# Listed orders for TensorE, ScalarE and VectorE in an attention and channel-mix kernel

## The chip, the core and the metric

The kernel runs on one core of one Trainium2 chip. The metric is the device time of one execution in microseconds (us). The time before is 232.12 us, the median of three runs (231.74 to 232.44). One further execution was recorded by the hardware profiler; it took 232.05 us, of which 230.3 us lie between its first and its last instruction (the span), and the durations in this document come from it.

A core has five engines that each take their instructions in a fixed order: TensorE (PE: matrix products, and PEld, the loads of its weights), VectorE (DVE), ScalarE (ACT), GpSimd (POOL) and SyncE (SP). In this kernel POOL does almost nothing but issue the loads, and SP issues the stores and the transposes by DMA.

## The reference

Two layers follow each other, on 8 sequences of 576 rows. The first is sliding-window attention with 8 heads of 64; the second is a channel mix that shifts each sequence by one row, with two weight matrices for a squared ReLU (512 to 1024 and back to 512) and one for a gate. All of it is computed, in float32 at the borders and bfloat16 inside.

```python
mask = (rel >= 0) & (rel < window)                       # window = 128
scores = where(mask, scale * q @ k.T + bias, -1e9)       # bias = -slope[h] * |rel|
x = softmax(scores) @ v                                  # B=8, H=8, S=576, D=64 -> (8, 576, 512)
x_prev = x shifted by one row, zeros first
xk = mu_k * x + (1 - mu_k) * x_prev
xr = mu_r * x + (1 - mu_r) * x_prev
out = sigmoid(xr @ w_r) * (relu(xk @ w_k)**2 @ w_v)
```

## The kernel before, in words

**Work.** Each batch b has four groups g of two heads. For a group TensorE makes transposes of q and k (qk_quad for batches 1 and 2, qk_some for 3 to 5; batches 6 and 7 are transposed by DMA), then scores (L729), which ScalarE turns into exponentials (L743) and VectorE multiplies with a mask (L756); then attend (L785), the product with v, which VectorE normalises (L791, L796); then a transpose back (out_t for batch 0, out_some for batches 1 to 5 at L840, DMA for 6 and 7). From the result VectorE makes xk and xr (L883, L890). The last 64 rows of each batch, its tails, are transposed apart: for batches 1 to 3 by four TensorE instructions (L915).

**The channel mix** is called 13 times, mix 0 to mix 12, each for a block of 256 to 512 rows. A mix has eight K operations (L994, four matmuls each, with ReLU on ScalarE at L1001 and the square at L967 on VectorE or L965 on ScalarE), and for every 128 rows one R operation (L1012, four matmuls, with tanh at L1019) and two V halves a and b (L1028, four matmuls each; VectorE makes the output ot from them at L1033, and SP stores it). "V mix0.0a" is the first half of the first 128 rows of mix 0. It needs the first half of w_v in wv_sb, and its half b needs the second.

**Loads.** POOL issues 113 loads in one fixed order. Counted from 0 they are: v of batch 0, w_k and parts of q and k (0 to 8), the rest of v and w_k (9 to 12), q and k of batch 1 (13 to 16) and its tails (17, 18), w_r (19), v of batch 1 (20 to 24), the halves of w_v (25, 26), q and k of batch 2 (27 to 30), its tails (31, 32) and v (33 to 37), then for every later batch q and k (38 to 45 for batch 3), tails (46, 47 for batch 3) and v.

**What sets the order.** No instruction is ordered at run time. The builder makes a list of operations with `plan.add`, each with the engines it may run on, a planned duration and latency, and the operations that it depends on. `Plan.run` plays the list through as events and emits every operation in the order of its planned start, so each engine's order, the buffer that each operation gets (`take`) and, for those that may run on ScalarE or VectorE, the engine, are settled before the kernel starts. Waits between engines are put in afterwards from the data. In `run`, a free engine takes from its ready operations the one with the smallest key. That key begins with a number of `PLACES`, one for each operation of TensorE, ScalarE and VectorE (L104 to L123). For TensorE `pe_key` changes it: while the array is split in two halves of 64 rows, operations of 64 rows go first. `paced` holds the transposes and scores of late batches until enough of the mixes has been planned. `dma` and `fab` plan the loads; `lat` is the planned latency of a transfer.

TensorE also runs 90 filler matmuls (L690) that write a scratch tile. Their key puts them behind everything else, so the plan takes them only where TensorE has nothing ready.

Of the kernel before, what the change touches and what calls it, by code (L numbers as in the profile page):

```python
# [21 lines left out]
PLACES = [int(x) for x in '''  # L22
# [54 lines left out]
'''.split()]  # L77


# [14 lines left out]
class Plan:  # L94
# [71 lines left out]
    def pe_key(self, n, rows):  # L166
        key = (n.place,) + tuple(n.prio)
# [1169 lines left out]
```

## Time and profile before

| | |
|---|---|
| median of three runs | 232.12 us |
| the profiled execution | 232.05 us, span 230.3 us |
| TensorE busy | 223.5 us (97% of the span) |
| VectorE busy | 187.7 us (82%) |
| ScalarE busy | 163.1 us (71%) |
| POOL busy | 93.9 us (41%) |
| granted TensorE clock | 1.000 |

Busy is the time in which at least one instruction of the engine is under way. A matmul's own duration is longer than the time until the next may start: a matmul of 512 columns lasts 379 ns, and the next starts 216 ns after it. So the time that an operation takes from TensorE is read from start to start, and is called its slot here. The word stall is used for slot time beyond what the same operation takes elsewhere. "Landing" is when the last part of a load has arrived.

### The profile page before, as it was taken

The page shows a single profiled execution, that of the slowest core. Times are in us where ns is not written, and L with a number is a line of the kernel's source. Part 1 is how long each engine was busy: PE and PEld are TensorE (multiplying, and loading weights), DVE is VectorE, ACT ScalarE, POOL GpSimd, SP SyncE. Part 2 cuts the span into 40 slices and gives each one's busy share as a digit, 9 for nine tenths or more (in the row PEclk, how much of TensorE's full clock was granted, in tenths as well). Part 3 has the DMA queues.
Part 4 walks back from the last instruction along what each step waited for, and adds up shares of the span by engine and source line. Part 5 has one row for each costly group of instructions (what it writes and reads, how often), then busy time and mean ns, then how long its engine had stood idle before and what let it go on. Part 6 is the DMA issues. An engine that isn't in the chain of part 4 may idle for free.

```text
span 230.3 us, 6675 instructions
## 1 busy us (share of the span) xinstructions
PE 223.5 (97%) x2715; PEld 135.2 (59%) x2715; DVE 187.7 (82%) x423; ACT 163.1 (71%) x295; POOL 93.9 (41%) x120
## 2 busy tenths in 40 slices
PE   8999998999999999999999999999999999999994
PEld 8675764765656656455655745545765544545552
DVE  8496998799949998997678997999999979563252
ACT  3769999599989969999797747959476455117421
POOL 8787654579976960991004961700000000000000
PEclk9999999999999999999999999999999999999999
DMA  6999999999999999999643999995230330231032
GB/s 169 183 168 197 189 161 198 193 176 156 189 141 170 160 145 184 96 144 185 141 117 38 173 180 156 131 136 182 78 86 3 137 103 37 89 129 52 3 137 91
DMA packets 121566, 31.11 MB, mean 135 GB/s; under 512 B 108216, under 2 KB 117696, under 8 KB 121536
## 3 DMA queue, kind: packets, MB, share of 16 engines
q0 software_dynamic: 96016, 16.26, 99.3%
q1 hardware_dynamic: 23776, 13.84, 24.0%
q10 hardware_dynamic: 1744, 0.59, 1.0%
q8 instruction: 21, 0.34, 0.6%
q14 instruction: 9, 0.07, 0.1%
HBM read 33.56 MB, written 9.44 MB: 187 GB/s over the span
## 4 chain that ended last, share of the span: by engine, by line
PE 79%; DMA 12%; POOL 4%; issue 2%; DVE 1%; ACT 0%; DVEq 0%; POOLq 0%
PE uno L994 25%; PE uno L1028 25%; PE uno L1012 13%; PE duo L785 7%; PE duo L729 6%; DMA wv_sb<-in_moe_w_v_dram 5%; DMA cb<-in_k_dram 4%; DMA wk_sb<-in_moe_w_k_dram 3%; PE uno L840 3%; POOL vs L503 1%; POOL cb L499 1%; POOL tv L508 1%; DVE ot L1033 1%; PE uno L1089 1%; DVE xr L890 0%
## 5 line engine op out<-in xcount | busy, mean ns | idle before, releaser
L994 PE MATMUL uno<-xk,wk_sb 128*128 128x256 bf16 (+2 forms) x416 | 72.4, 314 | 0.7 <-ACT qk L699 0.4
L1028 PE MATMUL uno<-wv_sb,kk 128*128 128x512 bf16 (+2 forms) x296 | 69.3, 374 | 1.1 <-DMA wv_sb<-in_moe_w_v_dram 1.0
L743 ACT ACTIVATE at<-duo 128x1024 bf16<-128x1024 f32 (+2 forms) x68 | 65.0, 1002 | 5.9 <-PE duo L729 5.5
L1001 ACT ACTIVATE rl<-uno 128x256 bf16<-128x256 f32 (+2 forms) x104 | 48.3, 496 | 25.7 <-PE uno L994 25.1
L994 PEld LDWEIGHTS <-wk_sb 128*128 128x128 bf16 x416 | 38.6, 98 | 23.4 <-issue 0.8
L503 POOL DMA_DIRECT2D vs<-in_v_dram x32 | 28.5, 906 | 40.5 <-PE duo L785 33.7
L1028 PEld LDWEIGHTS <-kk 128*128 128x128 bf16 x296 | 27.2, 98 | 29.7 <-issue 1.5
L756 DVE TENSOR_TENSOR at<-at,mask 128x1024 bf16<-128x1024 bf16 x56 | 37.2, 681 | 7.2 <-ACT at L743 7.2
L967 DVE TENSOR_TENSOR kk<-rl 128x256 bf16<-128x256 bf16 (+2 forms) x96 | 31.3, 337 | 12.5 <-ACT rl L1001 12.0
L1019 ACT ACTIVATE rs<-uno 128x512 bf16<-128x512 f32 x36 | 22.1, 617 | 21.5 <-PE uno L1012 13.2
L1012 PE MATMUL uno<-wr_sb,xr 128*128 128x512 bf16 x144 | 36.9, 380 | 0.0
L1033 DVE SCALAR_TENSOR_TENSOR ot<-rs,uno 128x512 f32<-128x512 bf16 (+2 forms) x37 | 24.2, 662 | 10.7 <-PE uno L1028 8.6
L699 ACT COPY qk<-uno 128x512 bf16<-128x512 bf16 (+1 forms) x41 | 21.8, 600 | 4.7 <-PE uno L1089 3.2
L890 DVE SCALAR_TENSOR_TENSOR xr<-dl,mu_sb,xt 128x576 bf16<-128x576 bf16 (+1 forms) x32 | 24.5, 774 | 0.0
L890 DVE SCALAR_TENSOR_TENSOR xk<-dl,mu_sb,xt 128x576 bf16<-128x576 bf16 (+1 forms) x32 | 24.4, 772 | 0.0
L785 PEld LDWEIGHTS <-at 128*128 128x128 bf16 x576 | 21.2, 98 | 5.0 <-issue 0.4
L796 DVE TENSOR_TENSOR xu<-duo,rc 128x640 bf16<-128x640 f32 x28 | 22.8, 817 | 0.9 <-DMA xt<-xu 0.5
L1012 PEld LDWEIGHTS <-xr 128*128 128x128 bf16 x144 | 13.3, 98 | 13.0
L534 POOL DMA_DIRECT2D cb<-in_k_dram x20 | 17.9, 919 | 4.9 <-DMA vs<-in_v_dram 2.9
L785 PE MATMUL duo<-vs,at 128*128 128x65 bf16 x448 | 19.0, 194 | 0.0
L534 POOL DMA_DIRECT2D cb<-in_q_dram x20 | 17.7, 938 | 0.8 <-PE uno L840 0.7
L699 ACT COPY xt<-uno 128x512 bf16<-128x512 bf16 (+3 forms) x28 | 15.2, 580 | 2.5 <-PE uno L823 1.5
(83 smaller groups left out, 202.8 us busy)
## 6 DMA issues: line engine op xcount, KB each, us to landing
out_dram<-ot SPq DMA_DIRECT2D x30, 256.0 KB, 3.3
vs<-in_v_dram POOLq DMA_DIRECT2D x32, 128.0 KB, 6.6
cb<-in_q_dram POOLq DMA_DIRECT2D x20, 128.0 KB, 6.6
cb<-in_k_dram POOLq DMA_DIRECT2D x20, 128.0 KB, 5.9
out_dram<-ot SPq DMA_DIRECT2D x10, 128.0 KB, 1.8
wk_sb<-in_moe_w_k_dram POOLq DMA_DIRECT2D x2, 512.0 KB, 7.2
cb<-in_q_dram POOLq DMA_DIRECT2D x4, 256.0 KB, 10.2
cb<-in_k_dram POOLq DMA_DIRECT2D x4, 256.0 KB, 10.5
```

Source lines behind the costliest of these rows:

```text
L503: return dma(POOL, 256, issue_t(1024), lambda e: nc.gpsimd.dma_start(out=vs_buf[h.idx][:, j, :, 0:D], in_=v[b, :, 128 * j:128 * j + 128].r ...
L534: return [dma(POOL, 256, issue_t(1024), lambda e, r=r: nc.gpsimd.dma_start(out=cb_buf[h.idx][:, i, r], in_=src[:, :, r]), [g], kind="q") f ...
L699: (nc.scalar.copy if e == ACT else nc.vector.tensor_copy)(out=out, in_=in_)
L743: lambda e, ah=ah, w=w, hp=hp: nc.scalar.activation(out=ah(), in_=two(hp)[:, :, 0:w], func=AF.Exp, scale=float(scale)), (), [hp])
L756: nc.vector.tensor_tensor(out=a, in0=a, in1=m, op=ALU.mult)
L785: nc.tensor.matmul(a[:, hl, t - t0], lhsT=at[:, lo:lo + 128], rhs=vs[:, u, 2 * g + hl, :] if u < NF else tvb[:, 2 * g + hl], start=(u == u ...
L890: lambda e: nc.vector.scalar_tensor_tensor(out=buf[hk.idx][:, g, e0 + c0:e0 + c1], in0=dls(), scalar=mu[:, g:g + 1], in1=xc(1), op0=ALU.mu ...
L967: nc.vector.tensor_tensor(out=out, in0=in_, in1=in_, op=ALU.mult)
L994: nc.tensor.matmul(one(hp)[:, 0:n], lhsT=wk_sb[:, po, 128 * fo:128 * fo + 128], rhs=xk_buf[hx.idx][:, po, c0:c1], start=(po == 0), stop=(p ...
L1001: a = op(ACT, act_t(n), [s], pr, lambda e, hp=hp, hr=hr: nc.scalar.activation(out=rl_buf[hr.idx][:, 0:n], in_=one(hp)[:, 0:n], func=AF.Rel ...
L1012: nc.tensor.matmul(one(hp), lhsT=xr_buf[hx.idx][:, po, 128 * c:128 * c + 128], rhs=wr_sb[:, po], start=(po == 0), stop=(po == NPO - 1))
L1028: nc.tensor.matmul(one(hv)[:, a:b], lhsT=kk_buf[hk.idx][:, fo, o:o + 128], rhs=wv_sb[:, fo, a:b], start=(fo == 0), stop=(fo == NFO - 1))
```

## The change

`PLACES` is replaced by `ORDER`, three lists of operation numbers: 425 for TensorE, 303 for ScalarE, 420 for VectorE, together 1148, numbered in the order of the calls of `plan.add` for these engines. `add` looks up the engine and the position of each operation, so that the engine of an operation that may run on two is given as well. In `run`, a free engine of these three may take only the operation whose position is its next turn; when that one isn't ready, the engine stays idle in the plan. `pe_key` and `paced` go. The fillers are in the list like any other operation.

In the plan, the landing of a POOL load is moved by a constant that depends on its number: -0.6 us for the first seven, +0.5 to +1.6 us for the next 35, +0.5 us for all later ones. POOL's and SP's order is still by `prio`, and the list of operations, their instructions and their data are the same. All of this is settled while the kernel is built.

```diff
+ORDER = {
+    "PE": [int(x) for x in """
+48 128 57 58 68 53 50 69 45 64 46 39 43 72 61 76 75 60 67 55 56 41 70 59 54 65 131 52 62 47 44 77 144 133 146 66
...
     def add(self, engs, dur, lat, deps, prio, emit=None, need=(), free=()):
         engs = (engs,) if isinstance(engs, str) else engs
+        place = None
+        if engs[0] in ORDER:
+            e, place = self.places[self.placed]
+            assert e in engs
+            engs = (e,)
+            self.placed += 1
...
-        n.place = 0
-        if emit is not None and engs[0] in ("PE", "ACT", "DVE"):
-            if prio[0] < 1e11:
-                n.place = PLACES[self.placed]
-                self.placed += 1
-            else:
-                n.place = 1 << 40
+        n.place = place
...
-    def pe_key(self, n, rows):
-        key = (n.place,) + tuple(n.prio)
-        if rows == 64 and n.rows[0] == 64:
-            return (-1e8,) + tuple(key)
...
-                    if e == "PE":
-                        cand.sort(key=lambda n: self.pe_key(n, rows))
+                    if e in turn:
+                        cand = [n for n in cand if n.place == turn[e]]
...
+                    if e in turn:
+                        turn[e] += 1
...
+        if queue == POOL:
+            i = last["loads"] = last.get("loads", -1) + 1
+            x = (-0.6 if i < 7 else 0.5 if i < 9 else 1.2 if kind in ("v", "tv") and i < 20 else 0.6 if i < 20
+                 else 1.6 if kind in ("v", "tv") else 1.1) if i < 42 else 0.5
+            lat = (lat[0], lat[1] + x)
...
-        t = op(PE, 0.0295 * 2 * NF * m, cl[b] + paced(b, g), prio + (3,), emit, hp + hq, [hc])
+        t = op(PE, 0.0295 * 2 * NF * m, cl[b], prio + (3,), emit, hp + hq, [hc])
```

Decoded into operations, the two TensorE lists hold the same work and differ in its order. Up to position 117, K mix0.1, they hold the same operations. Ahead of V mix0.0a the new list has K mix1.2, 1.5, 1.7, R mix1.0 and attend of batch 1 group 0, which came later, and no longer has K mix1.3, 1.4 and R mix1.1. Ahead of the tails of batch 3 it has V mix2.0a in addition, and lacks attend of batch 2 group 3 and qk_some of batch 3 group 0. Of the operations that may run on either engine, 25 change theirs: seven squares and seven copies come to ScalarE, four squares and seven copies leave it.

More of the change, by code (lines that the diff above doesn't have):

```diff
@@ L17 @@
 import heapq
-PLACES = [int(x) for x in '''
[54 rows of a table removed]
-'''.split()]
+ORDER = {
+    "PE": [int(x) for x in """
[16 rows of a table added]
+""".split()],
+    "ACT": [int(x) for x in """
[12 rows of a table added]
+""".split()],
+    "DVE": [int(x) for x in """
[16 rows of a table added]
+""".split()],
+}
 class Hold:
@@ L103, in __init__ @@
         self.nodes = []
+        self.places = {n: (e, i) for e, ns in ORDER.items() for i, n in enumerate(ns)}
         self.placed = 0
@@ L164, in give @@
             self.free[h.cls].add(h.idx + i)
-    def pe_key(self, n, rows):
-        key = (n.place,) + tuple(n.prio)
-        if rows == 64 and n.rows[0] == 64:
-            return (-1e8,) + tuple(key)
-        if rows == 128 and n.lazy:
-            return (key[0] + self.wait,) + tuple(key[1:])
-        return tuple(key)
     def run(self):
@@ L188, in run @@
         served = None
+        turn = dict.fromkeys(ORDER, 0)
         order = []
@@ L211, in run @@
                     else:
-                        cand.sort(key=lambda n: (n.place,) + tuple(n.prio))
+                        cand.sort(key=lambda n: n.prio)
                     for n in cand:
@@ L399, in dve_t @@
         return (n / fast + 66) / 960.0
-    AHEAD = 30.0
     NBIAS = 4
     XRL = 4.0
-    SLOPE = 4.7
     def op(e, dur, deps, prio, emit, need=(), free=()):
@@ L969 @@
     pe_mix = []
-    def paced(b, g):
-        want, k = (4 * b + g - AHEAD) * SLOPE, 0.0
-        for n in pe_mix:
-            k += n.dur
-            if k > want:
-                return [(n, 0.0)] if want > 0 else []
-        return []
     def channel_mix(P, c0, c1, first, xks, xrs, order):
@@ L1244, in emit_t @@
                         "p h d -> p (h d)"), ident)
-        t = op(PE, 0.0565 * 8, cl[b] + paced(b, g), prio + (3,), emit_t, [hp, hq], [hc])
+        t = op(PE, 0.0565 * 8, cl[b], prio + (3,), emit_t, [hp, hq], [hc])
         y = op(ACT, act_t(1024), [t], prio + (3,), lambda e: copy_any(
@@ L1259 @@
                 hq, y = xbh[b], xbl[b]
-                pace = paced(b, g)
+                pace = []
             else:
@@ L1263 @@
                 if b in WIDE:
-                    two_q[:] = [qk_quad(b, g, NF, lambda b=b: wide_buf[ch[b].idx], cw[b][g // 2] + paced(b, g),
+                    two_q[:] = [qk_quad(b, g, NF, lambda b=b: wide_buf[ch[b].idx], cw[b][g // 2],
                                         prio, 0, Hold("qk"), True, [ch[b]])]
```

97 rows, old and new, of tables (ORDER, PLACES) are left out of this document.

## The prediction

> **What bounds the kernel now.** I read the engines' shares first, then the busy time by stretch, then TensorE's waits, and then the timeline wherever a slot was too long.
>
> ```profile
> PE 223.5 (97%) x2715; PEld 135.2 (59%) x2715; DVE 187.7 (82%) x423; ACT 163.1 (71%) x295; POOL 93.9 (41%) x120
> ...
> core 0: us, PE busy (x) PEld busy (x) DVE busy (x) ACT busy (x) POOL busy (x), PEclk, DMA share, GB/s
> 0.00:20.00 20.00, 18.68 (x277) 13.62 (x278) 14.73 (x64) 12.36 (x23) 16.12 (x27) 1.00 1.44 178
> 20.00:37.76 17.76, 16.21 (x317) 11.92 (x316) 15.43 (x40) 17.54 (x40) 10.66 (x14) 1.00 1.73 182
> 37.76:62.15 24.39, 23.91 (x440) 15.26 (x440) 22.42 (x45) 20.64 (x41) 18.91 (x23) 1.00 1.97 182
> 62.15:227.10 164.95, 164.70 (x1690) 94.37 (x1686) 134.77 (x275) 112.56 (x195) 48.16 (x58) 1.00 1.09 118
> 227.10:230.30 3.20, 0.00 (x0) 0.00 (x0) 0.36 (x2) 0.00 (x0) 0.00 (x0) 1.00 0.32 115
> ```
>
> From 62.15 us to the last matmul TensorE has 0.25 us idle in 164.95: order can win almost nothing there. Idle time lies ahead of that, and in the first 37.76 us partly as fillers. Where TensorE waits:
>
> ```profile
> PE uno L1028 <- DMA wv_sb<-in_moe_w_v_dram: 1.0, 1, 1.0
> ...
> PE uno L994 <- ACT qk L699: 0.4, 1, 0.4
> PE uno L1089 <- ACT qk L699: 0.4, 1, 0.4
> ...
> PE uno L994 <- DVE ot L1033: 0.2, 1, 0.2
> ```
>
> From start to start these cost more than the idle time says: 0.59 us at 28.2, 1.17 ahead of V mix0.0a, 0.21 for the second half of w_v, 0.62 at 43.8, 0.38 at 205. In the timeline, V mix0.0a starts as its load lands, and the tails of batch 3 run at 62.15, well after their load 47 (issued at 55.08, 5.8 us to landing, so there at 60.84 by the unrounded times):
>
> ```profile
> 36.04 0.71 PE L994 MATMUL uno<-xk,wk_sb 128*128 128x256 bf16 x5
> 37.76 1.02 PE L1028 MATMUL uno<-wv_sb,kk 128*128 128x512 bf16 x4 [1.01 <-DMA wv_sb<-in_moe_w_v_dram]
> ...
> 62.15 0.39 PE L915 MATMUL uno<-ident,ts 128*128 128x128 bf16 x4
> ...
> 55.08 0.72 POOL L524 DMA_DIRECT2D ts<-in_k_dram  x1
> ...
> ts<-in_k_dram POOLq DMA_DIRECT2D x1, 64.0 KB, 5.8
> ```
>
> **The change part by part.** No instruction is added or dropped, so the price is TensorE's list laid against the landings. Slots from start to start in the trace: V half and R 0.86 us, K 0.86, 0.65 or 0.44 by its rows (512, 384, 256), attend 0.55, scores 0.45, qk_some 0.46, qk_quad 0.27, out_some 0.30, tails 0.22. A change between the whole and the halved array adds 0.10 (scores take 0.55 when a whole-array operation follows).
>
> *K mix0.1 to V mix0.0a.* Before: 15.55 us of slots from 19.80, and 2.41 of stalls. The new list has 1.00 more (attend 0.55, one more K 0.45): 16.55. Nothing can start V mix0.0a ahead of 37.71, when load 25 is there, so from the same 19.80 the new list has 1.41 us to spare, and gets 1.00 us of later work done in time that was stall. ScalarE (17.54 of 17.76 us busy) is the cover that could fail: its list from the first exponential of batch 0's second part to the last ReLU needed here is about 21.0 us of slots; from 15.85, where that stretch began before, it ends at 36.9. The spare is 0.9 us.
>
> *The start.* VectorE's list now has the scratch tile of the fillers third, and casts of the first q and k mixed with copies (0.17 to 0.34) and scalings (0.14). I bound it between 0.7 us earlier (a transpose at 14.00 and one at 14.74 stood behind fillers, and their loads landed at 13.12) and 0.6 later (the items between the casts). Both ends are inside the spare time above; I take 0.
>
> *V mix0.0a to the tails of batch 3.* Before: 8 V 6.91, 8 K 5.21, 3 K 1.34, 6 attend 3.29, 4 scores 1.81, 4 qk_quad 1.08, 2 out_some 0.60, R 0.86, tails 0.22, qk_some 0.46, 18 changes 1.80, sum 23.6; with 0.83 of stalls 37.76 + 24.4 = 62.2, the trace has 62.15. New: 9 V 7.77, 8 K 5.21, 2 K 0.89, 4 attend 2.20, 4 scores 1.81, 4 qk_quad 1.08, 2 out_some 0.60, R 0.86, tails 0.22, 12 changes 1.20, sum 21.85, so 59.6. But load 47 lands at 60.84: the tails start at 60.89, and 1.28 us go to waiting. Smaller waits on the way (quads of batch 2, load 30 at 45.62, wanted at 45.10; tails of batch 2, load 32 at 46.89, wanted at 46.34) lie inside that.
>
> *From there to the last matmul.* Before 164.59 us of slots. The new list has one attend (0.55), one qk_some (0.46) and two changes (0.20) more and one V half (0.86) less: 164.94. So the last matmul ends at 60.89 + 164.94 = 225.83, before at 227.07: 1.24 us less. The last four operations are the same in both lists, so the 3.20 us behind stay. From xk of batch 7 group 3, late at 205 before, the new VectorE list takes away the output operation that stood ahead of it (that 0.38 is in the comparison). What is late next is any load or handover with little to spare; later loads have 1.6 us (qk_some of batch 5) and more.
>
> *Where load 47 can land.* POOL issues 43 to 47 back to back once load 35 is there (51.27), and that one followed load 27, so TensorE's order hardly enters. POOL took up to 0.53 us after a landing to issue, elsewhere 0.28: at best 0.5 earlier, and then the tails of batch 2 hold the end at 225.13 (gain 1.94). At worst 8.5 us as the tails of batch 1 took: 63.6, a loss of 1.5. I take 60.84: both lists have the same four row blocks stored by then, so the traffic is alike.
>
> The DMA rule of the Trainium skill speaks against a hold there: "DMA: Bandwidth & Descriptors", section "Anatomy of one DMA — SWDGE (gpsimd) path", puts a transfer from the gpsimd queue at about 2.0 us and its bytes at 436 GB/s, estimated at 2.15 us for the 64 KB of load 47, so at 57.2; by it the tails would not wait and the gain would be 2.5 us. The trace has 5.8 us for that very load, so the sum stays with 60.84.
>
> *Engine moves.* Three squares net go to ScalarE, about 0.43 us busy each, and leave VectorE (0.28 each). ScalarE was idle from 41.1 to 43.8, and that covers them; without cover 1.3 us.
>
> *New stalls.* TensorE lost 0.38 us after 62.15 before, at one handover that had 0.23 us to spare by the same sums. In each list six results have less than 0.5 us to spare after 62.15, so I take 0.3 us. Sum: 232.05 - 1.24 + 0.3 = 231.1 us. The profiled execution lies 0.07 under the median, which I neglect.
>
> **The rivals.** *Not held at the tails* (loads earlier, or the skill's rule): bounded by V mix0.0a alone, 37.76 + 21.85 + 164.94 = 224.55, gain 2.5, 229.5 us. Against it: all loads around it took 4.4 us and more.
>
> *Hidden anyway*: the loads set both points, and ScalarE, VectorE or a landing 0.6 to 2.0 us later gives the gain back: 231.4 to 232.8 us, 232.1 in the middle. For it: VectorE is busy 22.42 of 24.39 us in the stretch that is to shrink by 1.3. Against it: TensorE had no stall on VectorE there, and ScalarE had 2.7 us idle.
>
> *Slower*: VectorE and ScalarE are held in order by an operation that waits. The trace shows it once:
>
> ```profile
> 200.49 0.45 DVE L883 TENSOR_TENSOR dl<-xt 128x576 bf16<-128x576 bf16 x1
> 202.88 0.69 DVE L1033 SCALAR_TENSOR_TENSOR ot<-rs,uno 128x512 f32<-128x512 bf16 x1 [1.94 <-issue]
> 203.49 0.81 DVE L890 SCALAR_TENSOR_TENSOR xr<-dl,mu_sb,xt 128x576 bf16<-128x576 bf16 x1
> ```
>
> xr and xk were ready, stood behind ot for 1.94 us, and TensorE lost 0.38. In the new list the six close results are squares of mix 5, 6, 7 and 11 behind rc or ot, and copies of batch 5, five of them from 110 to 147 us. If all six miss by 0.38, 2.3 us: 233.1 us. It decides from 1.94 us in all (1.24 and the bound of no change, 0.70). The skill's "TensorE: Matmul & The Clock Gate", table of specifications, says that ScalarE and VectorE take their queue strictly in order; the row above agrees. Against it: six as close results cost only 0.38 before.
>
> That the lists leave the work as it was is excluded: decoded, they differ in nearly every position.
>
> **How the numbers follow.** A change under 0.3% (0.70 us) can hardly be told from none. Forecast (230.8 to 231.4): 0.50. Not held: 0.07. Hidden: 0.26. Slower: 0.17. So faster 0.57, same 0.26, slower 0.17. The likeliest alone spans 230.8 to 231.4. The range goes from the early bound of load 47 (232.05 - 1.94 = 230.1) to the slower case, 233.1; the rest of not held and of slower, under 2 in 10, stays out.
>
> **What the profile would show.** Right: V mix0.0a within 0.1 us of its load and near 37.8; the tails of batch 3 (L915, third of its kind) at 60.9 right behind load 47; no stall at 43.8 or 205; TensorE's idle time after 62 under 0.6 us. Wrong, if V mix0.0a starts after 39, if load 47 lands elsewhere, or if TensorE waits for VectorE or ScalarE between 107 and 147 us.

## The result, and the profile after

The changed kernel takes 233.0 us, the median of nine runs (232.58 to 233.27), against 231.85 us (231.38 to 232.44) for nine runs of the kernel before: a ratio of 1.0041, with a 95% interval of 1.0026 to 1.0056. (The ratios in this document are not quotients of the two medians; they can differ from those by up to 0.2%.) The prediction was 231.1 us. The change makes the kernel 0.4% slower where it was forecast to make it faster. The time lies just inside the upper end of the range, 233.1, which came from another mechanism. The profiled execution took 233.0 us, with a span of 231.2 us.

The engines' shares and the busy time by stretch of the changed kernel, cut at K mix0.1, V mix0.0a, the tails of batch 3 and the last matmul, as the stretches shown of before (whose first cut, at 20.00, lies 0.20 us behind K mix0.1). The columns of a stretch are its ends, its length, and the busy time and number of instructions of each engine:

```profile
PE 221.5 (96%) x2681; PEld 135.3 (59%) x2715; DVE 189.0 (82%) x420; ACT 164.0 (71%) x298; POOL 93.5 (40%) x120
...
core 0: us, PE busy (x) PEld busy (x) DVE busy (x) ACT busy (x) POOL busy (x), PEclk, DMA share, GB/s
0.00:20.05 20.05, 18.07 (x275) 13.04 (x276) 14.64 (x62) 12.54 (x24) 15.25 (x26) 1.00 1.36 163
20.05:38.60 18.55, 17.26 (x343) 12.95 (x339) 14.74 (x40) 17.58 (x40) 11.15 (x15) 1.00 1.67 184
38.60:62.70 24.10, 22.66 (x369) 14.06 (x374) 22.47 (x41) 21.84 (x42) 18.83 (x23) 1.00 1.99 180
62.70:228.01 165.31, 163.47 (x1704) 95.26 (x1729) 136.74 (x279) 112.00 (x195) 48.24 (x58) 1.00 1.06 119
228.01:231.23 3.22, 0.00 (x1) 0.00 (x0) 0.40 (x2) 0.00 (x0) 0.00 (x0) 1.00 0.36 125
```

About thirty matmul records of the last long stretch are missing from this trace, so PE's busy time there says nothing of idle time; the ends of the stretches do. Laid against the prediction's sum:

| | forecast | measured | miss |
|---|---|---|---|
| K mix0.1 starts | 19.80 | 20.05 | +0.25 |
| V mix0.0a starts | 37.76 | 38.60 | +0.84 |
| tails of batch 3 start | 60.89 | 62.70 | +1.81 |
| last matmul ends, with 0.3 of new stalls | 226.13 | 228.01 | +1.88 |
| behind the last matmul | 3.20 | 3.22 | +0.02 |

From the tails of batch 3 on, the forecast held to 0.1 us (165.24 with its stalls, 165.31 measured). All of the miss lies ahead of it, in two pieces: 0.84 us until V mix0.0a, and 0.97 us from there to the tails.

**The first piece: a load that landed later.** POOL's queue and VectorE's, around the time when POOL comes to load 11, the tails of v (timeline of the changed kernel; the columns are start, duration, engine, line, operation, count, and in brackets the idle time before with what ended it):

```profile
11.94 0.90 POOL L498 DMA_DIRECT2D vs<-in_v_dram  x1 [0.88 <-DMA wk_sb<-in_moe_w_k_dram]
14.59 0.69 POOL L503 DMA_DIRECT2D tv<-in_v_dram  x1 [1.76 <-DVE tv L478]
15.28 0.76 POOL L539 DMA_DIRECT2D wk_sb<-in_moe_w_k_dram  x1
...
13.75 0.42 DVE L694 COPY qk<-uno 128x256 bf16<-128x256 bf16 x1
14.09 0.17 DVE L786 RECIPROCAL rc<-uno 128x4 f32<-128x4 f32 x1
14.23 0.07 DVE L478 MEMSET tv<- 64x8 bf16 x1
...
28.94 1.51 POOL L539 DMA_DIRECT2D wv_sb<-in_moe_w_v_dram  x2
```

The same in the kernel before:

```profile
7.15 0.07 DVE L483 MEMSET tv<- 64x8 bf16 x1
...
11.94 0.90 POOL L503 DMA_DIRECT2D vs<-in_v_dram  x1 [1.02 <-DMA wk_sb<-in_moe_w_k_dram]
12.92 0.69 POOL L508 DMA_DIRECT2D tv<-in_v_dram  x1
13.60 0.76 POOL L544 DMA_DIRECT2D wk_sb<-in_moe_w_k_dram  x1
...
27.46 1.51 POOL L544 DMA_DIRECT2D wv_sb<-in_moe_w_v_dram  x2
```

VectorE writes constants into the tv buffer that load 11 fills. One of these, operation 16, covers 64x8 elements in 0.07 us, and load 11 may not start before it. In the new list it stands at place 45 instead of 36, behind a copy of qk and a reciprocal, and runs at 14.23 instead of 7.15. POOL stands still for 1.76 us for it, and everything behind it in POOL's one queue comes later: load 12 by 1.7 us, and load 25 (the first half of w_v), which V mix0.0a reads, still by 1.48. It is issued at 28.94 and lands at 38.55 instead of 37.71. In this profile TensorE itself was ready for V mix0.0a only at about 38.54, since it had waited on the way for load 18 and for w_r, which had also moved; so the landing of load 25 and these waits set the point together.

**The second piece: TensorE stands with nothing to wait for.** In the 24.10 us from V mix0.0a to the tails there are 21.85 us of slots, as the prediction had them, and 2.25 us of stalls, none longer than this one (timeline):

```profile
49.98 0.60 PE L1015 MATMUL uno<-wv_sb,kk 128*128 128x512 bf16 x2
51.28 2.32 PE L1015 MATMUL uno<-wv_sb,kk 128*128 128x512 bf16 x9 [0.70 <-issue]
...
50.70 0.43 ACT L960 ACTIVATE kk<-rl 128x256 bf16<-128x256 bf16 x1
...
62.70 0.39 PE L910 MATMUL uno<-ident,ts 128*128 128x128 bf16 x4
```

The third matmul of V mix1.0a comes 1.30 us after the first, where the next but one comes 0.43 us after it elsewhere: 0.87 us are lost. The profile names no releaser ("issue"). The tails at 62.70 have no wait on their load: load 47 landed at 61.22. The rest of the 2.25 us is 0.43 at a quad of batch 2 (load 30 landed at 46.47), 0.33 at the tails of batch 2 (load 32, 48.00), 0.22 and 0.20 at two more places, and smaller ones. Loads 30 and 32 landed 0.86 and 1.11 us later than before, as load 25 did. That does not explain these stalls, though: in the kernel with both memsets early (below) the two loads landed at 45.26 and 46.42, ahead of before, and the stretch still took 23.99 us, 0.95 of it at V mix1.0a and about 1.2 at other places, where the profile names ScalarE's copies (ACT qk, ACT xt). What these 1.2 us hang on was not tested.

TensorE's waits from 20 to 64 us (total, times, longest) show the loads that had been no hindrance before, the tails of batch 1 (L910) and w_r:

```profile
PE uno L1015 <- issue: 0.7, 1, 0.7
PE uno L910 <- DMA ts<-in_k_dram: 0.6, 1, 0.6
PE uno L999 <- DMA wr_sb<-in_moe_w_r_dram: 0.4, 1, 0.4
PE uno L1076 <- ACT qk L694: 0.3, 1, 0.3
```

Two questions were open after this: whether the memset alone makes the first piece, and what the "issue" is.

### The profile page after: what moved, and what is told of

Read it like the earlier page. It is cut to its first block, busy times and chain, and to the rows that moved or that the text cites. A ratio compares the mean times of both kernels' runs of the same rounds, so it can differ in the third digit from the quotient of the medians.

```text
span 231.2 us, 6644 instructions
## 1 busy us (share of the span) xinstructions
PE 221.5 (96%) x2681; PEld 135.3 (59%) x2715; DVE 189.0 (82%) x420; ACT 164.0 (71%) x298; POOL 93.5 (40%) x120
## 4 chain that ended last, share of the span: by engine, by line
PE 84%; DMA 7%; POOL 2%; issue 2%; ACT 1%; DVE 1%; SPq 1%; DVEq 0%
PE uno L1015 27%; PE uno L981 26%; PE uno L999 13%; PE duo L724 6%; PE duo L780 6%; DMA wr_sb<-in_moe_w_r_dram 5%; PE uno L835 3%; DMA qx<-in_q_dram 2%; POOL cb L494 1%; ACT qk L694 1%; SPq L548 1%; POOL ts L519 1%; DVE ot L1020 1%; PE uno L685 1%; PE uno L1076 1%
## 5 line engine op out<-in xcount | busy, mean ns | idle before, releaser
L738 ACT ACTIVATE at<-duo 128x1024 bf16<-128x1024 f32 (+2 forms) x68 | 65.8, 988 | 7.4 <-PE duo L724 7.2
L1015 PE MATMUL uno<-wv_sb,kk 128*128 128x512 bf16 (+2 forms) x279 | 67.9, 373 | 1.9 <-issue 1.2
L988 ACT ACTIVATE rl<-uno 128x256 bf16<-128x256 f32 (+2 forms) x104 | 47.8, 480 | 30.9 <-PE uno L981 22.4
L962 DVE TENSOR_TENSOR kk<-rl 128x256 bf16<-128x256 bf16 (+2 forms) x93 | 29.8, 337 | 10.8 <-ACT rl L988 10.6
L999 PE MATMUL uno<-wr_sb,xr 128*128 128x512 bf16 x132 | 34.9, 379 | 1.3 <-DMA wr_sb<-in_moe_w_r_dram 0.4
L694 ACT COPY qk<-uno 128x512 bf16<-128x512 bf16 (+1 forms) x41 | 22.5, 598 | 4.8 <-PE uno L1076 2.7
L694 ACT COPY xt<-uno 128x640 bf16<-128x640 bf16 (+3 forms) x28 | 15.4, 585 | 1.3 <-PE uno L835 0.9
```

The source lines that it names most:

```text
L694: (nc.scalar.copy if e == ACT else nc.vector.tensor_copy)(out=out, in_=in_)
L738: lambda e, ah=ah, w=w, hp=hp: nc.scalar.activation(out=ah(), in_=two(hp)[:, :, 0:w], func=AF.Exp, scale=float(scale)), (), [hp])
L962: nc.vector.tensor_tensor(out=out, in0=in_, in1=in_, op=ALU.mult)
L988: a = op(ACT, act_t(n), [s], pr, lambda e, hp=hp, hr=hr: nc.scalar.activation(out=rl_buf[hr.idx][:, 0:n], in_=one(hp)[:, 0:n], func=AF.Rel ...
L999: nc.tensor.matmul(one(hp), lhsT=xr_buf[hx.idx][:, po, 128 * c:128 * c + 128], rhs=wr_sb[:, po], start=(po == 0), stop=(po == NPO - 1))
L1015: nc.tensor.matmul(one(hv)[:, a:b], lhsT=kk_buf[hk.idx][:, fo, o:o + 128], rhs=wv_sb[:, fo, a:b], start=(fo == 0), stop=(fo == NFO - 1))
```

## Experiments on the memset

**The memset back to the front.** Operation 16 goes right behind operation 15, the other constant of the same buffer. Only VectorE's list differs from the changed kernel's.

```diff
-... 23 15 33 19 35 ... 176 201 160 16 161 ...
+... 23 15 16 33 19 35 ... 176 201 160 161 ...
```

> The changed kernel with one operation moved: the small memset (64x8, 0.07 us) of the first tv buffer goes from place 45 of VectorE's list to place 25, right behind the large memset of the same buffer. Theory 'queue hold': that memset, late at 14.23, kept POOL's load 11 waiting 1.76 us, and every later load of the queue with it. Then load 11 is issued at about 12.9 in place of 14.59, load 25 (first half of w_v) at about 27.5 in place of 28.94, it lands near 37.7 in place of 38.55, V mix0.0a starts near 37.8 in place of 38.60, and the time falls by about 0.8 us, 232.9 to 232.1. Rival 'traffic': the landings are set by what the memory carries and by the stores and loads already under way, not by the issue; load 25 then lands within 0.3 us of 38.55 and the time stays at 232.8 to 233.1.

Measured: 232.07 us, 0.9989 of the kernel before (0.997 to 1.0008): not told apart from it, and clearly under the changed kernel's 1.0041. In the timeline the wait on VectorE is gone:

```profile
12.85 0.90 POOL L498 DMA_DIRECT2D vs<-in_v_dram  x1 [2.03 <-DMA wk_sb<-in_moe_w_k_dram]
13.82 0.69 POOL L503 DMA_DIRECT2D tv<-in_v_dram  x1
14.51 0.76 POOL L539 DMA_DIRECT2D wk_sb<-in_moe_w_k_dram  x1
```

In this one profile load 10 waits 2.03 us instead of 0.88 for load 2 of w_k, which landed at 12.56, so the marks behind it moved little: load 25 landed at 38.20, V mix0.0a started at 38.27 and the last matmul ended at 227.56, 0.45 us earlier than in the changed kernel. That the landing of one early load differs by 0.9 us here, and by 1.4 us between two profiles of the very same kernel (the repeat below), is a limit on all single marks; the ratios do not rest on it.

**The memset back in the kernel before.** The cross-check: the engines' orders of the kernel before, written as lists (every engine issues the same instructions in the same order as before), with operation 16 alone put later, behind operation 153, a difference dl of batch 0.

```diff
-(VectorE, kernel before) ... 17 21 16 167 ... 161 153 186 ...
+... 17 21 167 ... 161 153 16 186 ...
```

> The kernel before, its own order written as strict lists (the same instructions in the same order on all engines), with one operation moved: the same small memset goes from place 36 of VectorE's list to behind the difference of batch 0 group 1, so that it is done near 14.5 instead of 6.6. Nothing on TensorE, ScalarE or the queues is moved. Theory 'queue hold': load 11 is issued at about 14.6 (12.92 before), load 25 lands near 38.5 (37.71), V mix0.0a starts near 38.6 (37.76), and the time rises by about 0.8 us to 232.7. Rival 'traffic': load 25 lands within 0.3 us of 37.71 and the time stays within 0.2 us of the kernel before.

Measured: 233.16 us, 1.0036 (1.002 to 1.0053). Timeline:

```profile
15.03 0.69 POOL L502 DMA_DIRECT2D tv<-in_v_dram  x1 [1.48 <-DVE tv L477]
...
29.45 1.49 POOL L538 DMA_DIRECT2D wv_sb<-in_moe_w_v_dram  x2 [0.52 <-DMA ts<-in_q_dram]
...
38.74 1.02 PE L1014 MATMUL uno<-wv_sb,kk 128*128 128x512 bf16 x4 [0.33 <-DMA wv_sb<-in_moe_w_v_dram]
```

One instruction of 0.07 us, moved, makes the kernel before as slow as the changed one: V mix0.0a at 38.74 instead of 37.76, the span 231.28 instead of 230.30. In this profile load 2 landed 0.72 us later as well (12.37 instead of 11.65), so its marks hold more than the memset; the ratio does not rest on them. Taken out and put in, the memset moves the time by about the same amount, so it is enough for the loss against the kernel before. It does not explain why there is no gain.

**The other memset ahead of POOL's queue.** POOL's very first load waits in the changed kernel for operation 2, a constant in vs, and is issued at 2.75 instead of 2.22. Here operation 2 goes third in VectorE's list, on top of the first edit.

```diff
-1 3 0 28 6 36 34 25 2 29 ...
+1 3 2 0 28 6 36 34 25 29 ...
```

> The changed kernel with the early memset of the tv buffer, and with the memset of the first vs buffer (place 8 of VectorE's list, done at 2.45, for which POOL's first load waited 0.72 us) moved to place 2. Theory 'queue hold': POOL's first load is issued at about 2.2 in place of 2.75, the first seven loads with it, the first half of w_k lands up to 0.5 us earlier, and with it loads 10 to 25; V mix0.0a starts 0.2 to 0.5 us earlier than with the tv memset alone (38.27) and the time falls by as much. Rival 'traffic': the landings from 8 us on are set by what the memory carries: V mix0.0a moves by less than 0.15 us beyond what one profile differs from another (up to 0.3), and so does the time.

Measured: 232.06 us, 0.9988 (0.9969 to 1.0007). The whole queue moves forward:

```profile
2.09 2.01 POOL L498 DMA_DIRECT2D vs<-in_v_dram  x2
...
12.63 0.69 POOL L503 DMA_DIRECT2D tv<-in_v_dram  x1
...
48.95 0.61 PE L1015 MATMUL uno<-wv_sb,kk 128*128 128x512 bf16 x2
50.33 1.46 PE L1015 MATMUL uno<-wv_sb,kk 128*128 128x512 bf16 x6 [0.78 <-issue]
```

Load 25 landed at 37.25 and V mix0.0a started at 37.76, where the prediction had it. The tails of batch 3 then came at 61.75 and the last matmul ended at 227.06, which is where it ended in the kernel before (227.07). So with both memsets in place the first piece is gone, and the gain is still nothing: in the trace the second piece takes it. The matmul behind the "issue" comes 0.95 us late here, 0.87 in the changed kernel.

## Experiments on the stall without a releaser

**Is it the square?** In the changed kernel the stall ends at 51.28, just behind the square of K mix1.4 on ScalarE (50.70 to 51.13), which stands in ScalarE's list behind two copies. Put ahead of them it ends earlier; if TensorE stood for it, the stall must shrink.

```diff
-(ScalarE) 505 504 318 301 378 379 302 509
+505 504 318 301 302 378 379 509
```

> The changed kernel with one operation moved: the square of K mix1.4 stands right behind its ReLU in ScalarE's list, ahead of the two copies of xt of batch 1 group 3 (1.18 us together) that it stood behind. Theory 'in-order hold': V mix1.1a loses 0.87 us to that square; then it starts at about 50.85 in place of 51.71, the tails of batch 3 at about 61.8 in place of 62.69 (their load 47 is there at 61.22), and the time falls by 0.87 to about 232.1. Rival 'taken back': something right behind (the copies, now 0.4 us later, or a load) gives the time back before 62.7; then the tails of batch 3 stay within 0.3 us of 62.69 and the time at 232.7 to 233.1.

Measured: 233.01 us, 1.0036 (1.0018 to 1.0055), no better than the changed kernel. Timeline:

```profile
49.89 0.42 ACT L960 ACTIVATE kk<-rl 128x256 bf16<-128x256 bf16 x1
...
50.43 0.60 PE L1015 MATMUL uno<-wv_sb,kk 128*128 128x512 bf16 x2
52.01 1.24 PE L1015 MATMUL uno<-wv_sb,kk 128*128 128x512 bf16 x5 [0.97 <-issue]
```

The square was done at 50.31, and TensorE stood between the same two matmuls until 52.01. The square is refuted, and the profile names no other result that this matmul waited for.

**Both edits** (operation 16 and operation 302):

> Both moves together. If both theories hold and nothing new comes between, the tails of batch 3 are wanted at 62.69 - 0.84 - 0.87 = 60.98; load 47 was there at 61.22 in the changed kernel and at 60.84 in the one before, so they start between 61.0 and 61.3, the last matmul ends at 226.3 to 226.6 (before: 227.07) and the time is about 231.3 to 231.6, within 0.3% below the kernel before. If only one of the two counts, about 232.1; if none, 232.9.

Measured: 232.37 us, 0.9997 (0.9973 to 1.002), the same as with operation 16 alone within the intervals. The stall was there, until 51.16; V mix0.0a started at 38.56 and load 47 landed at 60.97.

**Instruction fetch.** In all of these kernels the stall is at the same instruction, whatever had run before it: 1729 instructions of TensorE stand ahead of it (1723 matmuls and weight loads and six semaphore and drain instructions of its queue). It is called instruction 1729 here, and the others are counted in the same way. The list of DMA queues of the changed kernel holds one that is not the program's:

```profile
q8 instruction: 21, 0.34, 0.6%
```

21 packets of 16 KB, and TensorE has 5430 matmuls and weight loads, which is 21 blocks of 256 and a rest. 1729 is 193 + 6 x 256. If TensorE's instructions come in blocks of 256 and one block comes late, the stall is bound to a place in the code and not to an operation. Then shifting the code must move it to another operation. Each dropped filler takes two instructions, a matmul and a weight load, out of the code ahead, and each one issued twice adds two. Eight fillers fewer, 32 fewer (58 in place of 82 below), and eight issued twice, each on top of the edit of operation 16; what the fillers compute is read by nothing.

```diff
-    NWARM = 90
+    NWARM = 82
```
```diff
+    def emit_warm2(e):
+        emit_warm(e)
+        return emit_warm(e)
-        plan.add(PE, ..., emit_warm, (), [h_wm])
+        plan.add(PE, ..., emit_warm2 if i in (10, 53, 61, 62, 63, 66, 71, 88) else emit_warm, (), [h_wm])
```

> The changed kernel with the early memset of the tv buffer, and with 8 of the 90 filler matmuls left out (they only keep TensorE busy between 7 and 14 us, where it waits anyway; nothing reads them). All later TensorE instructions move up by 16 places in the program. Theory 'code blocks': TensorE's program comes in blocks of 256 instructions (16 KB packets of the instruction queue); in the four kernels with the changed list TensorE stood still 0.7 to 1.25 us ahead of the third matmul of V mix1.0a, each time at instruction 1729 and 1.3 to 1.7 us after such a packet had ended, while nothing that the matmul reads was late. With 16 instructions fewer the block ends 16 instructions later in the work, where TensorE takes about 7.0 us for the 256 instructions before it in place of 5.6, and the fetch needs some 5.9 to 6.3: the stall there is under 0.2 us, and the tails of batch 3 start 0.4 to 0.8 us earlier than with the memset alone (62.24), unless load 47 (61.85 there) holds them. Time 0.2 to 0.8 us less than that kernel (232.07). Rival 'dependence': V mix1.0a itself waits for something; the stall of 0.6 to 1.1 us stays ahead of its third matmul, and the time stays.

> The same with 32 fillers left out: the blocks end 64 instructions later in the work. Theory 'code blocks': the stall at V mix1.0a goes (6.9 us for the 256 instructions), but the block that ended before it now ends among the transposes between 45.5 and 46.5, where TensorE takes only 3.9 us for 256 instructions: a new stall of 1.5 to 2.4 us there, at instruction 1473, and the time is 0.5 to 1.5 us above the kernel with the memset alone. Rival 'dependence': no stall over 0.6 us between 44.5 and 47, the one at V mix1.0a stays, and the time stays within 0.3 us.

> The changed kernel with the early memset of the tv buffer, and with 8 fillers issued twice: all later TensorE instructions move down by 16 places. Theory 'code blocks': the stall is again at instruction 1729, which is now 16 instructions earlier in the work, ahead of V mix1.0a (in scores of batch 2 group 3), 0.8 to 1.2 us long (5.35 us for 256 instructions), and V mix1.0a has none behind its second matmul. Time within 0.4 us of the kernel with the memset alone. Rival 'dependence': the stall stays ahead of the third matmul of V mix1.0a.

Measured:

| | us | ratio to before | stall ahead of V mix1.0a's third matmul | stall at the shifted block edge |
|---|---|---|---|---|
| 8 fillers fewer | 232.07 | 0.9997 (0.9974 to 1.0021) | none | none at 1729; 0.65 at 961 |
| 32 fillers fewer | 233.22 | 1.0038 (1.0012 to 1.0064) | none | 0.26 at 1473 |
| 8 fillers twice | 232.72 | 1.0012 (0.9989 to 1.0036) | none | 0.24 at 1729 |

With 32 fillers fewer and with eight issued twice (timelines; PEld are the weight loads):

```profile
45.85 0.32 PEld L834 LDWEIGHTS <-xu 64*128 64x128 bf16 x17 [0.38 <-issue]
```
```profile
49.60 0.11 PEld L729 LDWEIGHTS <-qk 64*128 64x128 bf16 x3 [0.25 <-issue]
...
49.82 2.27 PEld L1020 LDWEIGHTS <-kk 128*128 128x128 bf16 x12
```

961 and 1473 are 193 + 3 x 256 and 193 + 5 x 256. The place followed the code in all three: with eight twice, the stall came inside the scores of batch 2 group 3, at the same instruction number, and V mix1.0a ran through. A cause tied to the operation is refuted. The new stalls at 1473 and 1729 were far smaller than I had expected (0.26 and 0.24 us), so the place is settled and the size is not. The stretch from V mix0.0a to the tails took 23.12 us with eight fewer and 23.28 with eight twice, against 23.97 with all fillers, so the shift gives back 0.7 to 0.9 us there.

The gain did not reach the medians, and why is open. With eight fewer, the profiled execution was the slowest of its twelve (234.04 us): TensorE stood idle for 0.90 us and 0.48 us at 13 to 14.7, waiting for loads of q and k where fillers had been, and the granted clock was low behind that (timeline, and busy time by stretch; the clock is the third number from the end, 0.58, and it was 0.99 and 1.00 in the 4 us ahead and behind):

```profile
13.92 0.26 PE L1076 MATMUL uno<-ident,qx 64*64 64x64 bf16 x8 [0.90 <-DMA qx<-in_q_dram]
...
16.00:20.00 4.00, 4.00 (x60) 2.23 (x57) 2.48 (x8) 2.55 (x7) 3.54 (x5) 0.58 1.44 142
```

K mix0.1 started at 22.57 in that profile. The clock does not explain the median: over the whole execution the mean granted clock was 0.993 in this one and 0.998 or more in the other eleven. With 32 fewer, 0.69 us were lost at 175.48, where the profile names a ReLU of ScalarE, and the time is 1.15 us over that of operation 16 alone; most of that is unexplained. With eight twice the profiled execution took 231.97 us, but the median is 232.72, 0.65 over operation 16 alone and outside the 0.4 expected; that is unexplained too.

**The code shifted, the clock kept.** Eight fillers fewer, and eight of the remaining ones 256 columns wide, so that TensorE works as long as before. The edits of operations 16 and 2 are in.

```diff
-    NWARM = 90
+    NWARM = 82
-    warm = cst.tile([128, 128], BF16, name="warm")
+    warm = cst.tile([128, 256], BF16, name="warm")
+    def emit_wide(e):
+        nc.tensor.matmul(one(h_wm)[:, 0:256], lhsT=warm[:, 0:128], rhs=warm, start=True, stop=True)
-        plan.add(PE, ..., emit_warm, (), [h_wm])
+        plan.add(PE, ..., emit_wide if i in (63, 65, 67, 69, 71, 73, 75, 77) else emit_warm, (), [h_wm])
```

> The changed kernel with both memsets early, with 8 fillers left out and 8 others twice as wide (256 columns), so that TensorE is kept as busy as before while all that follows stands 16 instructions earlier in the program. With 8 fillers merely left out TensorE's granted clock had dropped to 0.58 between 16 and 20 us behind a gap of 0.90 us, which hid what the shift did. Theory 'code blocks': no such drop; no stall over 0.2 us at V mix1.0a or V mix1.1a (1.06 with both memsets early and no shift); a stall of 0.3 to 0.7 us near 31 us, where a block now ends in the dense transposes of batch 1, and V mix0.0a at 37.8 to 38.3; from V mix0.0a to the tails of batch 3 23.0 to 23.3 us in place of 23.99; time 0.3 to 0.9 us below the one with the memsets alone (232.06), 0.2 to 0.5% below the kernel before. Rival 'taken back': the stall goes, and the loads or VectorE take the time back before 62 us; then the stretch stays at 23.7 or more and the time within 0.1% of the kernel before.

Measured: 231.85 us against 232.06 for the kernel before, 0.9987 (0.9972 to 1.0002). Timeline:

```profile
30.27 0.32 PE L1080 MATMUL uno<-ident,cb 64*64 64x64 bf16 x17 [0.57 <-issue]
...
49.32 2.55 PE L1019 MATMUL uno<-wv_sb,kk 128*128 128x512 bf16 x10
...
61.44 0.38 PE L914 MATMUL uno<-ident,ts 128*128 128x128 bf16 x4
```

The clock was full throughout. V mix1.0a runs through, and a new stall of 0.76 us stands at instruction 961, ahead of V mix0.0a, where about half of it falls into the spare time before load 25 (landed at 37.67, V mix0.0a at 38.06). The tails of batch 3 now stand behind load 47, which landed at 61.30: the profile names no releaser, but they start 0.1 us behind the landing, as the tails of batch 1 did in the changed kernel (28.33 and 28.43). So in this profile the hold that the prediction had put there shows, once nothing else is later. The last matmul ended at 226.74 and the span was 229.96, 0.3 us under the kernel before. The time is clearly under the changed kernel's, and its interval does not quite exclude no change against the kernel before. The theory had asked for 0.2 to 0.5% below it. The ratio is that of the kernel with the memsets alone (0.9988) and of operation 16 alone (0.9989), so the 0.3 us that the trace shows for the shift are not shown by the times.

**R mix1.1 one place earlier**, ahead of the quad of batch 2 group 3 that waits for load 30 (on top of the last kernel):

```diff
-(TensorE) 346 503 317
+346 317 503
```

> The same, and R mix1.1 goes ahead of the transposes of batch 2 group 3 on TensorE, so that it runs while they wait for load 30 (0.36 us) and the tails behind them for load 32 (0.12 to 0.24). If these waits count: scores of batch 2 group 3 start 0.3 to 0.5 us earlier, the tails of batch 3 are wanted near 60.6, where load 47 lands, and the time is another 0.2 to 0.5 us less, 231.0 to 231.4, 0.3 to 0.6% below the kernel before. If VectorE (xk of batch 1 group 3, at 53.2) or load 47 holds instead, the time is as without this move within 0.2 us.

Measured: 232.06 us, 0.9998 (0.9981 to 1.0014). The stretch from V mix0.0a to the tails took 23.00 us with 0.93 us of stalls, so 22.07 without, against the prediction's sum of 21.85. The last matmul ended at 226.63, 0.11 us earlier than without the edit, and the median does not show it.

## Experiments on the order, and a repeat

**Later work first.** On top of the edits of 16 and 2, TensorE's order from 45 to 54 us: R mix1.1, K mix1.4 and the tails of batch 2 go ahead, the quad of batch 2 group 3 behind V mix1.0b, its scores behind V mix1.1b; ScalarE and VectorE follow. The output of this kernel is wrong: by the lists, VectorE sets the border of one attention buffer to zero only after batch 2 has first read it, so part of batch 2 is computed from other values. The instructions are the same, so their waits can be read all the same. In the second, in addition, the tails of batch 3 come three operations later.

```diff
-(TensorE) 346 503 317 459 300 377 506 314 319 315 492 475 320
+346 317 300 459 377 314 319 315 503 492 475 320 506
-(ScalarE) 505 504 318 301 378 379 302 509 507 494 478 476
+318 301 302 378 379 505 504 494 478 476 509 507
```
```diff
-(TensorE) 412 567 599 464 420 410
+412 599 464 420 567 410
```

> The changed kernel with both memsets early, and with the operations between 45 and 54 us in another order: the transposes (quads) of batch 2 group 3 go from ahead of R mix1.1 to behind V mix1.0b, next to those of group 2; K mix1.4 stands ahead of the tails of batch 2; scores of batch 2 group 3 go behind V mix1.1b; the square of K mix1.4 right behind its ReLU; ScalarE's copies and exponentials and one mask of VectorE follow that order. Theory 'code blocks' with the waits of the list: the 256 instructions before instruction 1729 now take about 6.4 us in place of 5.6, so the stall there (1.06 us with both memsets early) is under 0.3; no wait for load 30 (0.36), and under 0.2 for load 32. K mix2.0 is then bound by VectorE's xk of batch 1 group 3 at about 53.0 in place of 54.38, the tails of batch 3 are wanted near 60.45 and start near 60.6 as load 47 lands (61.75 with the memsets alone), and the time is about 231.0 us, 0.4 to 0.6% below the kernel before. Rival 'ScalarE and VectorE in order': the new order makes copies, exponentials or masks late between 50 and 60 us, K mix2.0 or the K behind it wait, the tails of batch 3 stay within 0.4 us of 61.75 and the time within 0.2% of the kernel before.

> The same, and the tails of batch 3 (with their copy on VectorE) stand three operations later, behind R mix2.2, so that load 47 can hold nothing. Theory 'held at the tails' (the hold that the prediction put there): the last matmul ends 0.2 to 0.6 us earlier than in the kernel without this move, and the time is 230.4 to 230.9 us. Rival: load 47 holds nothing there, and the two are the same within 0.2 us in the trace.

Measured: 234.3 us, 1.0106 (1.0089 to 1.0123), and 235.31 us, 1.015 (1.013 to 1.0169). TensorE's waits from 44 to 64 us in the first of them (total, times, longest):

```profile
PE duo L724 <- ACT at L738: 1.7, 2, 1.1
PE uno L1076 <- ACT qk L694: 1.2, 1, 1.2
```

TensorE waits for ScalarE, far longer than in the kernel with both memsets early (0.2 us twice in the same stretch): for copies at the quads and for exponentials at the scores. That fits the "Slower" rival of the prediction, ScalarE and VectorE in order behind something that is not ready, at another place and in another order than it was expected. In the second the tails came at 65.86, though their load was there at 60.6; in the first they had come at 64.01 with the load there at 60.52, so load 47 held nothing in either, and the pair says nothing of the hold. The stall at the block edge was gone here, with 256 instructions that took 8.2 us instead of 5.6.

**The changed kernel once more**, to see how far a profile and a median repeat:

> The changed kernel itself once more, beside the two on the same chip. It shows how much one profile differs from another without any edit: V mix0.0a 38.3 to 39.2, the stall at instruction 1729 0.6 to 1.3 us, the tails of batch 3 near 62.7 to 63.4, and a ratio to the kernel before of 1.0026 to 1.0056 as measured at first.

Measured: 232.99 us, 1.0051 (1.0027 to 1.0075): the median repeats to 0.01 us, closer than this interval gives reason to expect. The profile does not: K mix0.1 at 21.15, V mix0.0a at 39.80, the span 232.3, with load 2 at 13.01 instead of 11.65. One profile of this kernel can lie 1.1 us from another, from the landing of one load on. The stall at instruction 1729 was there again, 0.78 us.

## Why the prediction was wrong

Two steps failed. The sum had the profiled execution 0.94 us shorter (1.24 less 0.3), and it missed by 1.88: 0.84 up to V mix0.0a, and 0.97 from there to the tails. One of them alone takes about the whole gain; both together make it a loss.

**The start, taken as 0, with "Nothing can start V mix0.0a ahead of 37.71, when load 25 is there": this step failed by 0.84 us.** I bounded the start by what TensorE takes from VectorE's new list, the casts and copies. I did not ask what POOL takes from it. POOL's order is the same in both kernels, and I read that as the loads being the same. But two of POOL's loads wait for VectorE, for constants of 0.07 us and the like, and one of those moved nine places back in VectorE's list. The landing of load 25 was used as a fixed point, and it was the point that moved, by 0.84 us. The 1.41 us of spare time that I had counted went too: between K mix0.1 and V mix0.0a TensorE took the 16.55 us of slots as summed, and 2.00 us of stalls, 0.83 of them at load 18 and 0.48 at w_r, whose landings had moved by 1.5 us each.

**V mix0.0a to the tails: the slots were right, what lay beside them was not.** 21.85 us of slots were summed; the changed kernel had 24.10 us with 2.25 of stalls, and without its stalls the same. The forecast left 1.28 us for waiting, at load 47 or before it, so 0.97 are over. The sum had no term for TensorE having no instruction to run: 0.87 us at instruction 1729. I read the stretch before, which has no such stall, as though the price of an order depended only on operations and data.

**The hold at the tails of batch 3 at 60.89.** The tails started at 62.70, past load 47 (61.22 instead of 60.84), so the hold was covered by the two pieces above. With the memsets early and the code shifted it appeared: 61.44, behind a landing at 61.30. But this landing is no fixed point either: it lay between 59.25 (R mix1.1 earlier) and 63.01 (the repeat) in the profiles.

**From the tails to the end** was right: 164.94 plus 0.3 of new stalls against 165.31, and 165.30 to 165.33 in nine of the experiments (165.9 with 32 fillers fewer). The bet on the six close results (0.3 us, not 2.3) fits that as well, and the "Slower" rival's place between 107 and 147 us did not come into play. ScalarE in the first stretch held, as the cover that I had named.

**"Hidden anyway"** described the total best: its 231.4 to 232.8 us, a landing 0.6 to 2.0 us later giving the gain back, ends 0.2 us short of the measured 233.0. I gave it 0.26. The "Slower" rival has nearly the measured time, 233.1, by six waits for ScalarE and VectorE between 107 and 147 us that the changed kernel does not show; so it is luck that the range reaches 233.0. What the first piece shows is of the same kind at another place: a memset held in VectorE's order, for which POOL waited, not TensorE.

**The rule of the Trainium skill on a transfer from POOL's queue** ("DMA: Bandwidth & Descriptors", section "Anatomy of one DMA — SWDGE (gpsimd) path", about 2.0 us) does not hold in this stretch: load 47 took 5.5 us from issue (55.72) to landing (61.22), near the 5.8 of before.

## What to carry to other kernels

When the order of one engine's instructions changes, list every instruction on it that another queue waits for, the tiny ones first: a memset of 0.07 us that stands ahead of a load in an in-order queue of loads moves every load behind it. A landing in the profile of before is a fixed point only for as long as all that the loading queue waits for stays in place. And when one engine's stalls have no releaser, look whether they stand at the same instruction number in every order, and move when instructions are added ahead of them, before looking for data.

## What the runs showed of the hardware

**TensorE's code arrives in blocks of 256 instructions, and a dense stretch can outrun it.** From the trace, for the block edge at instruction 1729; "edge before" is when TensorE passed instruction 1473, the packet is the 16 KB transfer on the instruction queue:

| kernel | edge before | packet | matmul behind the edge | stall |
|---|---|---|---|---|
| before | 45.15 | 46.91 to 48.33 | 51.44 | none |
| changed | 44.87 | 49.04 to 50.00 | 51.28 | 0.87 |
| operation 16 | 44.44 | 48.55 to 49.50 | 50.83 | 0.6 |
| operation 302 | 45.39 | 49.64 to 50.61 | 52.01 | 1.15 |
| both | 44.85 | 48.59 to 49.55 | 51.16 | 0.94 |

In these rows the packet starts after the edge before has been passed, 1.8 to 4.3 us behind it, lasts 1.0 to 1.4 us, and where TensorE stood, the first instruction behind the edge came 1.3 to 1.6 us after the packet's end. In the four that stood that is 6.3 to 6.6 us in all for 256 instructions. The new order puts many 64x64 transposes, two short instructions each, between the two edges, and needs only about 5.6 us for them; the order before takes over 6. That the stall belongs to a place in the code is shown by the kernels with shifted code; that the block comes late there is inferred from the packet's times. That the lag between edge and packet comes from the loads that are in flight is an idea only. It was 2.4 to 5.1 us in most blocks of the first 60 us; later on packets started between 1.7 us ahead of the edge and 4.3 us behind it. What sets it stays open, and with it the size of any such stall.

The Trainium skill ("Runtime: NRT & Kernel Launch", section "Instruction fetch mechanics") says that the code is refilled in blocks of 16 KiB, 256 instructions, while the current one runs, and that the cost of crossing an edge is mostly hidden. The blocks agree with the 21 packets here. The cost agrees with most of the edges and not with this one: 0.6 to 1.15 us in the five kernels that keep the new order and the code's place (these four, and 0.95 with both memsets early).

**A granted clock of 0.58 over 4 us, cause open.** In one execution of the kernel with eight fillers fewer, idle gaps of 0.90 and 0.48 us within 1.7 us were followed by that clock. With a gap of 0.47 to 0.49 us at the same place in three other kernels it stayed full, and so it did with gaps of 0.82 and 0.43 us in the repeat of the changed kernel (timeline, and busy time by stretch):

```profile
13.82 0.26 PE L1076 MATMUL uno<-ident,qx 64*64 64x64 bf16 x8 [0.82 <-DMA qx<-in_q_dram]
...
16.00:20.00 4.00, 4.00 (x84) 2.21 (x80) 3.65 (x12) 3.53 (x9) 4.00 (x6) 1.00 0.95 77
```

So it is not shown that gaps of this size cost the clock, nor that the fillers, which compute nothing, are worth their time here.
